# Gate, up and W_down regrouped by every fourth column, and wo's end loaded in quarters, in a decode kernel

## The chip, the cores and the metric

The kernel runs on one core of one Trainium2 chip. The metric is the device time of one execution in microseconds. A comparison runs both kernels in alternation on the same chip. Beside the time, each run gives its span: the time from the first to the last instruction in the records. The profile is of one execution, and its clock starts at the span's start.

## The reference

One decode step of a pre-norm block: two batch elements, one query token each, 32 heads, 8192 cached keys and values for each head, head size 128, then a gated MLP with 512 inputs and 1376 hidden columns. Everything is bf16.

```python
def _A_ref(x, k_cache, v_cache, wq, wo):        # cut: reshapes
    q = (x @ wq).reshape(B, Sq, Hq, Dh)
    scores = jnp.einsum("bhqd,bhkd->bhqk", q, k) * (Dh ** -0.5)
    p = _softmax(scores, axis=-1)
    o = jnp.einsum("bhqk,bhkd->bhqd", p, v)
    return o.reshape(B, Sq, Hq * Dh) @ wo
def _B_ref(x, W_gate, W_up, W_down):
    gate = jnp.einsum("bsd,df->bsf", x, W_gate)
    up = jnp.einsum("bsd,df->bsf", x, W_up)
    h = gate * (gate > 0) * up                  # cut: dtype casts
    return jnp.einsum("bsf,fd->bsd", h, W_down)
h = x + _A_ref(_layernorm(x), k_cache, v_cache, wq, wo)
h2 = h + _B_ref(_layernorm(h), W_gate, W_up, W_down)
```

## The kernel before

The caches are 268 MB (2 x 2 x 32 x 8192 x 128 elements of two bytes), so the kernel is a long stream of loads. A loop of 16 rounds handles four heads a round: VectorE multiplies keys with the query and adds them up, ScalarE takes the exponentials, TensorE applies the values. Behind the last cache load the SyncE queue holds wo, W_gate, W_up and W_down, in the order in which they are needed. The loads of that tail:

```python
for k in range(NGR):                            # wo in two halves of 2 MB
    s.dma("sp", f"dwo{k}", lambda k=k, r0=r0: sync.dma_start(
        out=wo_sb[:, k * JG:(k + 1) * JG, :]..., in_=A_wo[r0:r0 + NS * G * Dh, :]...
# ... gate, up (3 of 4 chunks), up (the last chunk)
for f, r in blocks:                             # W_down: 4, 4 and 2 rows for each of 128 partitions
    s.dma("sp", f"dwd{f}", lambda f=f, r=r: sync.dma_start(
        out=wd_sb[:, f:f + r, :].rearrange("p r n -> p (r n)"),
        in_=B_W_down[f * P:(f + r) * P, :].rearrange("(p r) n -> p (r n)", r=r)), ...
s.dma("sp", "dwdl", lambda: sync.dma_start(out=wd_l, in_=B_W_down[FULL:F, :]), ...)   # last 96 rows
```

Gate and up are matrix products with the two batch elements in the stationary operand, made in three column tiles of 512 columns (the third overlaps the second); then their product is turned into columns and multiplied with W_down:

```python
def mlp_in(g, ps, c0, c1):
    for c in range(c0, c1):
        for j in range(FT):                     # FT = 3
            last = pe.matmul(out=ps[j * Q:(j + 1) * Q, :],
                             lhsT=hd[:, c].rearrange("p a b -> p (a b)"),
                             rhs=wgu[:, g, c, offs[j]:offs[j] + MT], ...)
# ... product, columns_of_act
for f0, r in blocks:
    def fn(f0=f0, r=r):
        for f in range(f0, f0 + r):
            last = y_rows(act_t[:, f, :], wd_sb[:, f, :])     # four matmuls of 128 columns
        return last
    s.op("pe", fn, reads=["act_t", f"wd{f0}"], writes=["y"])
s.op("pe", lambda: y_rows(act_t[0:LASTW, NF, :], wd_l, last=True), ...)
```

The softmax here doesn't subtract the row's maximum and nothing guards it: scores larger than these inputs give would overflow.

## Time and profile before

| what | value |
|---|---|
| time, median of 3 runs | 660.19 us (660.06 to 660.62) |
| span of the profiled run | 658.7 us |
| DMA packets of the load queue, share of 16 engines' span | 98.9% |
| VectorE busy | 618.0 us, 94% |
| one round of the loop, by the value loads' landings | 38.70 us |

The first view is the page of the kernel before: busy time, share of the span and instructions of each engine; the busy tenths of the DMA engines in 40 slices; and the queues that moved data, with packets, megabytes and share.

```profile
PE 115.0 (17%) x1234; PEld 47.3 (7%) x1234; DVE 618.0 (94%) x184; ACT 59.4 (9%) x155; POOL 3.8 (1%) x15
...
DMA  9999999999999999999999999999999999999996
...
q1 hardware_dynamic: 6456, 281.06, 98.9%
q8 instruction: 3, 0.05, 0.0%
q14 instruction: 3, 0.02, 0.0%
```

The DMA row is 9 in every slice but the last. VectorE's 94% looks like a second limit, but it is the lesser one: in the loop it keeps up with the loads, and it waits 4.6 us in all for keys. The two small queues at the bottom fetch instructions.

The second view is the chain of waits of the kernel before, the part at the end: start, duration, what it was.

```profile
621.36 22.94 DMA v<-in_A_wo_dram
...
644.43 1.91 PE mm L596 x13
...
646.36 0.73 DVE osb L611
...
648.55 1.76 PE o L654 x12
...
650.72 1.85 PE mm L654 x12
...
652.66 0.69 DVE qrep L674
...
654.12 1.37 PE y L645 x44
...
655.51 0.29 DVE sc L711
```

Read it as a ladder. The second half of wo lands at 644.29; 16 matmuls finish the attention output, VectorE transposes it, gate, up, their product, and 44 matmuls with W_down follow, and at 655.51 the result is cast for the output. No load but wo is in it: in this kernel the end is bound by its own computing. The last of W_down landed at 654.60, in time for the last of the 44 matmuls.

The third view is the timeline of the kernel before: start, duration, engine, line, operation, tiles, shapes, count; in brackets the idle time before and what ended it.

```profile
644.43 1.87 PE L596 MATMUL mm<-v 128*2 128x512 bf16 x16 [3.05 <-DMA v<-in_A_wo_dram]
...
648.42 1.90 PE L654 MATMUL o<-k,sc 128*32 128x512 bf16 x12
...
650.65 1.89 PE L654 MATMUL mm<-k,sc 128*32 128x512 bf16 x12
...
654.12 1.34 PE L645 MATMUL y<-k,v 128*2 128x128 bf16 x44 [0.28 <-ACT v L696]
```

The last line: all 44 matmuls run in one go and wait for ScalarE, not for a load.

### The profile page before, as it was taken

The page shows a single profiled execution, that of the slowest core. Times are in us where ns is not written, and L with a number is a line of the kernel's source. Part 1 is how long each engine was busy: PE and PEld are TensorE (multiplying, and loading weights), DVE is VectorE, ACT ScalarE, POOL GpSimd, SP SyncE. Part 2 cuts the span into 40 slices and gives each one's busy share as a digit, 9 for nine tenths or more (in the row PEclk, how much of TensorE's full clock was granted, in tenths as well). Part 3 has the DMA queues.
Part 4 walks back from the last instruction along what each step waited for, and adds up shares of the span by engine and source line. Part 5 has one row for each costly group of instructions (what it writes and reads, how often), then busy time and mean ns, then how long its engine had stood idle before and what let it go on. Part 6 is the DMA issues. An engine that isn't in the chain of part 4 may idle for free. (4 is left out here: it accounts for less than half of the span.)

```text
span 658.7 us, 3100 instructions
## 1 busy us (share of the span) xinstructions
PE 115.0 (17%) x1234; PEld 47.3 (7%) x1234; DVE 618.0 (94%) x184; ACT 59.4 (9%) x155; POOL 3.8 (1%) x15
## 2 busy tenths in 40 slices
PE   2200302003030110303011030300203030020365
PEld 1000100001010000101000010100001010010122
DVE  1799999999999999999999999999999999999972
ACT  2301010010101001010100101010010101001100
POOL 2000000000000000000000000000000000000000
PEclk9655655656565575656557565565756556575655
DMA  9999999999999999999999999999999999999996
GB/s 378 447 446 414 418 446 442 446 438 394 446 442 442 442 402 438 442 442 442 410 430 442 442 442 414 426 442 442 442 434 406 446 442 438 438 406 442 418 421 248
DMA packets 6474, 281.13 MB, mean 427 GB/s; under 512 B 738, under 2 KB 836, under 8 KB 1348
## 3 DMA queue, kind: packets, MB, share of 16 engines
q1 hardware_dynamic: 6456, 281.06, 98.9%
q8 instruction: 3, 0.05, 0.0%
q14 instruction: 3, 0.02, 0.0%
q10 hardware_dynamic: 12, 0.00, 0.0%
HBM read 281.05 MB, written 0.00 MB: 427 GB/s over the span
## 5 line engine op out<-in xcount | busy, mean ns | idle before, releaser
L364 DVE TENSOR_TENSOR k<-k,qrep 128x32768 bf16<-128x32768 bf16 (+3 forms) x18 | 275.9, 15327 | 4.6 <-DMA k<-in_A_k_cache_dram 4.6
L370 DVE TENSOR_TENSOR k<-k 128x4096 bf16<-128x4096 bf16 (+6 forms) x72 | 267.4, 3714 | 2.5
L406 PE MATMUL o<-v,pm 128*32 128x512 bf16 x960 | 83.9, 526 | 466.9 <-PEq L434 466.9
L383 ACT ACTIVATE pm<-sc 32x256 bf16<-32x256 f32 (+2 forms) x68 | 48.2, 709 | 562.9 <-DVE sc L227 562.1
L406 PEld LDWEIGHTS o<-v,pm 128*32 128x32 bf16 x960 | 35.2, 127 | 515.3 <-issue 508.4
L227 DVE TENSOR_REDUCE sc<-k 128x256 f32<-128x2048 bf16 (+2 forms) x17 | 36.7, 2160 | 0.8 <-PE o L406 0.3
L453 DVE TENSOR_REDUCE osb<-om 128x128 f32<-128x512 f32 x16 | 16.5, 1029 | 0.6
L383 ACT ACTIVATION_READ_ACCUMULATOR pm<-sc 32x1 f32 x68 | 15.8, 233 | 0.0
L349 DVE CAST qrep<-mm 32x512 bf16<-32x512 f32 x4 | 2.8, 696 | 11.1 <-PE mm L333 11.1
L449 DVE TENSOR_TENSOR om<-o,turn_of 128x512 f32<-128x512 f32 x16 | 10.9, 681 | 1.8 <-PE o L406 1.8
L413 PE MATMUL rep<-osb,spread 128*32 128x128 f32 x40 | 3.9, 420 | 48.4 <-DVE osb L453 45.0
L406 PE MATMUL o<-k,pm 128*32 128x512 bf16 x64 | 7.4, 628 | 7.7 <-ACT pm L383 5.3
L333 PE MATMUL mm<-v,om 128*64 128x512 bf16 x32 | 6.6, 572 | 8.7 <-DMA v<-in_A_wq_dram 8.5
L346 ACT ACTIVATE qrep<-mm 32x512 bf16<-32x512 f32 x12 | 7.0, 587 | 9.1 <-PE mm L333 8.9
L611 DVE STREAM_TRANSPOSE osb<-mm 128x512 f32<-128x512 f32 x1 | 0.7, 717 | 6.7 <-PE mm L596 6.7
L413 PEld LDWEIGHTS rep<-osb,spread 128*32 128x32 f32 x40 | 1.4, 146 | 50.9 <-DVE osb L453 46.6
L596 PE MATMUL mm<-v 128*2 128x512 bf16 x32 | 3.7, 620 | 3.0 <-DMA v<-in_A_wo_dram 3.0
L522 POOL TENSOR_TENSOR zm<-zm,zx 128x1 f32<-128x1 f32 x1 | 0.2, 191 | 627.5 <-ACT pm L383 627.5
L333 PEld LDWEIGHTS mm<-v,om 128*64 128x64 bf16 x32 | 2.5, 152 | 12.4 <-issue 10.3
L406 PEld LDWEIGHTS o<-k,pm 128*32 128x32 bf16 x64 | 2.0, 133 | 12.7 <-ACT pm L383 6.7
L301 DVE COPY xc<-st 128x8 f32<-128x8 f32 x1 | 0.2, 165 | 2.6 <-PE st L296 2.6
L654 PE MATMUL o<-k,sc 128*32 128x512 bf16 x12 | 1.9, 628 | 0.0
(81 smaller groups left out, 33.3 us busy)
## 6 DMA issues: line engine op xcount, KB each, us to landing
k<-in_A_k_cache_dram SPq DMA_DIRECT2D x2, 4096.0 KB, 26.8
v<-in_A_wq_dram SPq DMA_DIRECT2D x1, 4096.0 KB, 12.3
k<-in_A_v_cache_dram SPq DMA_DIRECT2D x1, 4096.0 KB, 31.4
v<-in_A_wo_dram SPq DMA_DIRECT2D x2, 2048.0 KB, 20.4
k<-in_A_v_cache_dram SPq DMA_DIRECT2D x1, 3072.0 KB, 38.3
k<-in_B_W_gate_dram SPq DMA_DIRECT2D x1, 1376.0 KB, 14.9
k<-in_B_W_up_dram SPq DMA_DIRECT2D x1, 1032.0 KB, 17.1
k<-in_A_v_cache_dram SPq DMA_DIRECT2D x1, 1024.0 KB, 40.4
```

Of the source, the lines that this page charges most:

```text
L227: s.op("dve", lambda: dve.tensor_reduce(out=out_, in_=in_, axis=axis, op=ALU.add), reads=reads, writes=writes)
L333: last = pe.matmul(out=ps[h * B * Q:(h + 1) * B * Q], lhsT=xnb[:, c].rearrange("p b q -> p (b q)"), rhs=wq_h[:, c, g:g + QP, h0 + h, :], s ...
L346: s.op("act", lambda src=src, dst=dst: act.activation(out=dst, in_=src, func=ACT.Copy), reads=[f"mm{t}"], writes=[key])
L349: s.op("dve", lambda src=src, dst=dst: dve.tensor_copy(dst, src), reads=[f"mm{t}"], writes=[key])
L364: s.op("dve", lambda: dve.tensor_tensor(out=kp, in0=kp, in1=_view(qrep[:, b, i, :], 0, [[0, hi - lo], [1, Dh]]), op=ALU.mult), reads=keys ...
L370: s.op("dve", lambda half=half, width=width: dve.tensor_tensor(out=kp[:, :, 0:half], in0=kp[:, :, 0:half], in1=kp[:, :, half:width], op=AL ...
L383: last = act.activation(out=p_of[ps, lo // TG:hi // TG, :, h], in_=sc[ps, lo:hi].rearrange("p (g t) -> p g t", t=TG), func=ACT.Exp, accum_ ...
L406: last = pe.matmul(out=o[g:g + W2], lhsT=pm[:, t // TG, :], rhs=vs[:, t:t + TG, :].rearrange("p t d -> p (t d)"), start=(t < P // Q * TG), ...
L413: return pe.matmul(out=rep_ps[u * Q:(u + 1) * Q, :], lhsT=spread.rearrange("k h m -> k (h m)"), rhs=osb[:, u, :], start=True, stop=True, s ...
L449: s.op("dve", lambda: dve.tensor_tensor(out=om.rearrange("p (t d) -> p t d", d=Dh), in0=o.rearrange("p (t d) -> p t d", d=Dh), in1=_view(t ...
L453: fn = lambda: dve.tensor_reduce(out=osb[:, u, :], in_=om.rearrange("p (t d) -> p d t", d=Dh), axis=AXIS.X, op=ALU.add)
L596: last = pe.matmul(out=ar_ps[g:g + B], lhsT=oc[:, k, :], rhs=wo_sb[:, k, :], start=False, stop=(k + P // Q >= NK), skip_group_check=True)
```

## The change

The intent is a shorter computing chain at the end. wo's second half is loaded as a half and two quarters, so that only 4 of its 16 matmuls remain after the last landing. Gate and up are made in four column tiles, tile j holding the columns j, j+4, j+8 and so on: 344 instead of 512 columns for each matmul, with nothing done twice. The hidden columns then stand in fours, so W_down is loaded as rows of four. 344 rows of four are 2 x 128 + 32 + 56; the last 56 (224 rows of W_down) go in eight loads of seven partitions each, so that only seven DMA engines carry them. Masks are built on GpSimd, scores have two buffers, the input x is loaded a second time, from ScalarE's queue, and some waits and some small VectorE operations go.

```diff
+    WO = ((0, 0, JG), (1, 0, JG // 2), (1, JG // 2, JG * 3 // 4), (1, JG * 3 // 4, JG))
+    for k, lo, hi in WO:
# ... the loads of wo and the attention matmuls follow these pieces
-        red(head_blk, ident.rearrange("p (h m) -> p h m", h=G), AXIS.X, i, ["head"])
# ... row_of and eye_of likewise: now copies and memsets on GpSimd; sc has two buffers
-    for f, r in blocks:
-        s.dma("sp", f"dwd{f}", ... 
-    s.dma("sp", "dwdl", lambda: sync.dma_start(out=wd_l, in_=B_W_down[FULL:F, :]),
+    s.op("pool", lambda: pool.memset(wd_sb[0:2 * Q, 2 * FT:], 0.0), writes=["wd2"], extra=x_free)
+    load_down("wd0", 0, slice(0, P), 0)
+    load_down("wd1", P, slice(0, P), FT)
+    load_down("wd2c", 2 * P, slice(2 * Q, 3 * Q), 2 * FT)
+    for h in range(2):
+        for m in range(4):
+            rest.append(f"wd2{h}{m}")
+            load_down(rest[-1], 2 * P + Q + h * 4 * NE + m,
+                      slice(h * Q + m, h * Q + m + 4 * NE - 3, 4), 2 * FT, [cleared])
-    for g in range(B * NGR - 1):
-        normalize(*divmod(g, NGR))
# ... one VectorE operation in place of two normalizations
-                                 rhs=wgu[:, g, c, offs[j]:offs[j] + MT],
+                                 rhs=wgu[:, g, c, j:F:FT],          # FT = 4
# ... the y matmuls of h move behind gate
-    for f0, r in blocks:
-    ...
-    s.op("pe", lambda: y_rows(act_t[0:LASTW, NF, :], wd_l, last=True), ...
+    for u in range(2):
+        s.op("pe", lambda u=u: add_y(u, P), reads=["act_t", f"wd{u}"], writes=["y"])
+    s.op("pe", lambda: add_y(2, 3 * Q), reads=["act_l", "wd2", "wd2c"] + rest, writes=["y"])
```

## The prediction

> **What bounds the kernel now.** The DMA engines. The DMA row of the 40 slices reads 9 everywhere but at the end, the queue's packets fill 98.9% of 16 engines' span, 281 MB pass at 427 GB/s, and from the trace's packets at least 16 are in flight at every moment sampled from 530 to 651 us. VectorE is close behind (618.0 us busy, 94%) and waits 4.6 us in all for keys. So in the loop (38.70 us a round by the value loads' landings) a faster VectorE only waits longer: nothing from the second score buffer, the masks on GpSimd, the dropped waits.
>
> **The end** is two races. The chain of waits follows one: second wo load lands 644.29, 16 matmuls 644.43 to 646.3, transpose 646.36, gate 648.42, up 650.65 to 652.54, product 652.66, columns 653.40, ACT copy 653.87, 44 down matmuls 654.12 to 655.49, cast 655.51, then some 3 us of output. The other is DMA: last increments of gate 647.61, up 650.09 and 650.99, W_down 652.49, 653.79, 654.40, 654.60. Three engines are late (last load: 653.93, 653.99, 654.60 against 652.3 to 653.2).
>
> **What the change does there**
> - wo in quarters: 4 instead of 16 matmuls after the last landing; a round of four takes 0.427 us, so 1.28 us less. But 8 KB and 4 KB packets move at 26.2 and 25.0 bytes/ns against 26.7 for 16 KB (packet medians): about +0.24 us on every later landing.
> - Gate and up: four rounds of 344 instead of 512 columns, 0.287 instead of 0.427 us: 0.56 us less each, if reading every fourth column is free. [...] Product and columns shrink by an estimated 0.4 us.
> - The y matmuls of h move behind gate: 0.43 us of PE, hidden while up is awaited.
> - W_down: 48 instead of 44 matmuls (+0.11 us). After the second block the late engines carry 8 KB instead of 22 KB in small packets, 0.33 instead of 0.95 us. The 224 rows cost seven engines 8 x 0.17 us; [...] The trace names no engines; I assume these seven are early ones.
>
> **Sum.** Compute gets some 2.6 us shorter, but runs into the loads: gate waits for its landing (about 647.85), up for 650.3, and the down matmuls, ready by about 653.0 instead of 654.1, stall for the second W_down block, 653.79 + 0.24 = about 654.03. After it 32 matmuls (0.86 us issue, 0.2 drain): cast at about 655.26 instead of 655.51. Only 0.25 us stays; the rest becomes waiting for DMA.
>
> Predicted: 659.9 us, range 659.0 to 660.8 (8 in 10). Faster by over 2%: 1%; within 2%: 98%; slower: 1%.
>
> **What would show it.** Loop round 38.70 as before; attention matmuls after wo 0.6 instead of 1.9 us; gate starting on a DMA, rounds of 0.29 us; a W_down load as the chain's last DMA; y matmuls split by a wait of some 0.8 us; last landing near 654.2.
>
> **What would make it wrong.** [...] one of the seven engines a late one (+1 us); instruction fetches, which I take to be what makes three engines late (16 KB at 27 and 635 us, 8 KB at 177, 199, 638), falling elsewhere (0.3 to 0.6 us either way).

The sum came to 659.9 us, 660.19 less the 0.25 us by which the cast moves.

## The result, and the profile after

The first comparison gave a median of 661.43 us for the changed kernel (660.86 to 661.63, six runs) against 660.39 us for the kernel before (660.06 to 660.85, six runs). The ratio was 1.0014, with a 95% interval of 1.0001 to 1.0027. A ratio here is the mean time of one kernel's fast runs over that of the other's of the same rounds, so not quite the ratio of the medians. A repetition among the experiments gave 1.0011 (0.9997 to 1.0024). By these ratios the change costs 0.7 to 0.9 us, 0.1% of the time; the second interval just holds 1. It was predicted to gain 0.3.

The page after, the lines that answer to those of before:

```profile
PE 114.0 (17%) x1244; PEld 47.1 (7%) x1244; DVE 617.2 (94%) x180; ACT 59.4 (9%) x155; POOL 7.7 (1%) x29
...
DMA  9999999999999999999999999999999999999996
...
q1 hardware_dynamic: 6648, 281.06, 98.9%
q8 instruction: 3, 0.05, 0.0%
q14 instruction: 2, 0.02, 0.0%
```

The same bytes in more packets, a little less VectorE work, and one instruction fetch fewer inside the span. The loop's round is 38.70 us, as before. The chain of waits after, its end:

```profile
627.13 2.30 DVE k L380
641.94 12.88 DMA k<-in_B_W_down_dram
```

The last link of the chain is now a load of W_down. From the moment of its issue the chain goes back through SyncE, which issues the MLP loads one after another from 632.62 us on, to VectorE's work on the last keys, because the MLP weights may only be written into that buffer when the keys have been read. The issuing is not what holds the end: the last eight loads were issued 0.74 us apart but landed 0.18 us apart. The timeline after:

```profile
644.13 0.60 PE L617 MATMUL mm<-v 128*2 128x512 bf16 x4 [0.66 <-DMA v<-in_A_wo_dram]
...
647.55 1.42 PE L676 MATMUL o<-k,sc 128*32 128x344 bf16 x16 [1.16 <-DMA k<-in_B_W_gate_dram]
...
650.00 1.42 PE L676 MATMUL mm<-k,sc 128*32 128x344 bf16 x16
...
652.84 0.39 PE L667 MATMUL y<-k,v 128*2 128x128 bf16 x16 [0.40 <-DMA k<-in_B_W_down_dram]
...
653.95 0.39 PE L667 MATMUL y<-k,v 128*2 128x128 bf16 x16 [0.72 <-DMA k<-in_B_W_down_dram]
...
654.95 0.39 PE L667 MATMUL y<-k,v 96*2 96x128 bf16 x16 [0.61 <-DMA k<-in_B_W_down_dram]
655.40 0.29 DVE L731 CAST sc<-y 128x128 bf16<-128x128 f32 x1 [2.75 <-PE y L667]
```

Nearly every step is shorter, and nearly every step now has a load in its brackets. Step by step, from the starts in the two timelines and the landing of the last piece of wo in the records (644.29 before, 644.08 after):

| step | before, us | after, us |
|---|---|---|
| last wo landing to transpose | 2.07 | 0.69 |
| transpose to gate | 2.06 | 2.78 |
| gate to up | 2.23 | 2.45 |
| up to product | 2.01 | 1.54 |
| product to first W_down matmul | 1.46 | 1.30 |
| first W_down matmul to cast | 1.39 | 2.56 |
| sum | 11.22 | 11.32 |

Attention saves 1.38 us, and the chain is 1.3 us ahead at the first W_down matmul (652.84 against 654.12, of which 0.2 came from wo). Nearly all of it is lost in the last row, in waits for W_down. From the cast to the end of the span it takes 3.65 us after and 3.23 before. Of that, 0.38 us is one thing: VectorE's last drain instruction began 0.49 us after the semaphore instruction in front of it, where it was 0.11 us before (in these profiles the gap is always one or the other).

Here are the landings of the W_down loads, by the last increment of each load's semaphore:

| load | before | after |
|---|---|---|
| first 128 partitions x 4 rows | 652.49 | 652.70 |
| second 128 x 4 rows | 653.79 | 653.90 |
| before: 128 x 2 rows; after: 32 partitions x 4 rows | 654.40 | 654.34 |
| before: 96 rows; after: the eighth seven-partition load | 654.60 | 654.82 |

### The profile page after: what moved, and what is told of

Same layout as the page of the kernel before. It is cut to its first block, busy times and chain, and to the rows that moved or that the text cites. A ratio compares the mean times of both kernels' runs of the same rounds, so it can differ in the third digit from the quotient of the medians.

```text
span 659.0 us, 3129 instructions
## 1 busy us (share of the span) xinstructions
PE 114.0 (17%) x1244; PEld 47.1 (7%) x1244; DVE 617.2 (94%) x180; ACT 59.4 (9%) x155; POOL 7.7 (1%) x29
## 4 chain that ended last, share of the span: by engine, by line
DVE 74%; DMA 24%; SPq 1%; issue 1%; PE 0%
DVE k L374 34%; DVE k L380 33%; DMA k<-in_A_k_cache_dram 22%; DVE sc L229 5%; DMA k<-in_B_W_down_dram 2%; SPq L549 1%; DVE osb L463 1%; DVE om L459 1%; SPq L540 0%; PE y L667 0%; SPq L283 0%; DVE ou L229 0%; DVE sc L731 0%; DVE rep L475 0%; SPq L770 0%
## 5 line engine op out<-in xcount | busy, mean ns | idle before, releaser
L416 PE MATMUL o<-v,pm 128*32 128x512 bf16 x960 | 85.8, 536 | 465.6 <-PEq L444 465.6
```

The source lines that it names most:

```text
L416: last = pe.matmul(out=o[g:g + W2], lhsT=pm[:, t // TG, :], rhs=vs[:, t:t + TG, :].rearrange("p t d -> p (t d)"), start=(t < P // Q * TG), ...
```

## The experiments

A late engine, here, is a DMA engine that ends its share of every load well after the others: in the kernel before, three engines ended the last load at 653.93, 653.99 and 654.60 us, and the others by 653.18.

Three explanations stood after the first look. Theory W: the W_down part costs the time; its last landing is later than before, because loads into few partitions are slow, or because one of the seven engines is a late one. Rival R: the rest of the change costs it, above all fewer VectorE instructions, which may put an instruction fetch on the last drain (the 0.38 us). And within theory W theory P stood against a rival H. Theory P says that packets are slow when several DMA engines write into few, close partitions; H says that the last rows of W_down are slow to read, wherever they are written.

All edits are against the changed kernel unless it says otherwise. "Before" is always the median or mean of nine runs of the kernel before on the same chip: medians 660.59, 660.59, 660.29 and 660.49 us for the four groups of runs.

### First group: repetition, fourteen engines, the fetch moved back, wo alone

The changed kernel again, no edit.

> The changed kernel unchanged, once more, to learn how its executions spread and to get a second trace. If the two profiled executions (658.7 before, 659.0 after) are typical, the changed kernel is 0.3 us slower, not the 1.0 us that the medians say. If the 1.0 us is real, its usual span is 659.5 to 659.8 and this trace, unlike the first, should show what takes the other 0.5 us, in the last 25 us.

Measured: 661.04 us (660.67 to 661.76), ratio 1.0011 (0.9997 to 1.0024), mean +0.59 us. In its profile the last W_down landing was 655.00, the cast 655.59, and the last drain again began 0.49 us after its release. So the loss repeats, with the sign and about the size of the first comparison.

Fourteen engines for the last 56 rows, two loads of 28 partitions:

```diff
-        for m in range(4):
-            rest.append(f"wd2{h}{m}")
-            load_down(rest[-1], 2 * P + Q + h * 4 * NE + m,
-                      slice(h * Q + m, h * Q + m + 4 * NE - 3, 4), 2 * FT, [cleared])
+        rest.append(f"wd2{h}")
+        load_down(rest[-1], 2 * P + Q + h * 4 * NE, slice(h * Q, h * Q + 4 * NE), 2 * FT, [cleared])
```

> The last 224 rows of W_down in two loads of 28 partitions (14 engines each) instead of eight of 7 partitions. Theory A: the seven engines are a bad choice, because one of them is itself late: its eighth row of 4 KB lands 654.82, 0.48 us after the latest engines had finished (654.34). With 14 engines each has four rows, about 0.74 us. If both latest engines are outside the fourteen, the last landing is near 654.35, the cast starts near 654.95 instead of 655.40, the time falls 0.45 us. If one is inside, the last landing is near 655.05 and the time rises 0.2 us. Rival B (instruction fetch of VectorE at the end): no change from this but what the landing gives.

Measured: 661.63 us, ratio 1.0018 (1.0004 to 1.0032). The last landing was 655.53. All three late engines took part in these loads; the two engines that did not are not late. And the packets became slow: a packet took up to 2.1 times its usual time between 651.25 and 653.25. The 28 partitions of each of these loads lie side by side.

Nineteen small VectorE instructions added at the start, so that VectorE has about as many as in the kernel before and its instruction fetches fall where they fell:

```diff
     build_masks()
+    for _ in range(19):
+        s.op("dve", lambda: dve.tensor_copy(zx, eps_t), reads=["eps"], writes=["zx"])
```

> The changed kernel with 19 tiny VectorE copies in the prologue, where VectorE idles, so that it has as many instructions as before. Theory B: the 8 KB instruction fetch that came at 638.6 us before and at the end after moves back into the run, VectorE's last drain comes 0.11 us after its release as before, not 0.49 us, and the span falls by up to 0.35 us, less what the fetch costs a DMA engine near 640 us (up to 0.3 us). Theory A: no change.

Measured: 661.62 us, ratio 1.0019 (1.0005 to 1.0033). The drain's gap was 0.11 us again, so the stall goes with the number of VectorE instructions. Two 8 KB fetches moved with that number too: they were at 177.2 and 659.4 us in the changed kernel and at 63.5 and 638.2 here, which is how they are taken to be VectorE's. Amid the loads such a fetch took 0.31 to 0.33 us in the traces of the kernel before and of the changed kernel. That a fetch is what holds the drain is not shown: the one at 659.4 us began 0.7 us after the held drain had started (658.72), and after the end of the span (659.05). But the time got worse, not better. In its timeline:

```profile
654.16 0.40 PE L669 MATMUL y<-k,v 128*2 128x128 bf16 x16 [0.76 <-DMA k<-in_B_W_down_dram]
656.04 0.39 PE L669 MATMUL y<-k,v 96*2 96x128 bf16 x16 [1.49 <-DMA k<-in_B_W_down_dram]
```

One engine delivered its eight rows of the seven-partition loads at 654.62, 654.81 and so on to 655.91, a row every 0.18 us; the other six were done by 654.19. With the fetch back at 638 us, one of the seven engines is the latest of all. Without it, in the changed kernel, the same loads end at 654.82.

The quarters of wo alone, in the kernel before:

```diff
-    for k in range(NGR):
+    WO = ((0, 0, JG), (1, 0, JG // 2), (1, JG // 2, JG * 3 // 4), (1, JG * 3 // 4, JG))
+    for k, lo, hi in WO:
...
-    attention_rows(NK - JG, NK, False)
+    for k, lo, hi in WO[1:]:
+        attention_rows(k * JG + lo, k * JG + hi, False)
```

> The kernel before with the second wo load in three pieces (8, 4 and 4 columns of rows) and nothing else. As I costed it: transpose 1.3 us earlier, gate then waits for its own landing, the down matmuls for W_down, so the cast comes 0.2 to 0.4 us earlier. If small packets cost what I said, every later landing is 0.24 us later and nothing or little is gained; the changed kernel's trace already says that they do not (last wo landing 644.08, not 644.53).

Measured: 660.32 us, ratio 0.9998 (0.9985 to 1.0012). The transpose started at 644.92 instead of 646.36, but the last W_down landing was 654.58, as before, and the cast came at 655.03, so about 0.5 us was left in this profile and 0.2 us in the mean of the times. The kernel before had that much room and no more before it would meet its last load.

### Second group: which engine, and two repairs

The 56 rows in loads of 7, 6, 5, 4, 3, 3 and 7, 6, 5, 4, 2, 2, 2 partitions, one row for each engine, to see which engine is the late one:

```diff
-    for h in range(2):
-        for m in range(4):
+    for h, counts in ((0, (7, 6, 5, 4, 3, 3)), (1, (7, 6, 5, 4, 2, 2, 2))):
+        at_row = 0
+        for m, k in enumerate(counts):
```

> A measurement, not a version: the 56 partition rows of the last 224 rows in loads of 7, 6, 5, 4, 3, 3 and 7, 6, 5, 4, 2, 2, 2 partitions[...]. Theory A says that one of the [...] engines is late by 0.7 us or more [...]. A load that includes it has one increment that stands apart from the others by that much; the first k whose load has no such increment names the engine. If no load shows one, the lateness belongs to the partitions or the row stride and not to an engine.

Measured: 661.93 us, one run, state unknown; an engine that takes part in all thirteen loads carries thirteen rows here, so the time itself says nothing. How many engines carry a load is read from its semaphore: in the trace of the changed kernel that of the first seven-partition load has one record at 637.82 us, long before its data moves, and then the seven increments from 652.43 to 653.52 us, as data lands. In the nested kernel the increments agree with the counts of partitions; loads over eight and sixteen partitions are counted alike below, one engine to a partition. The loads of the first half show how a late engine is found, last increments in us:

```
load over 7 partitions: 653.81      over 4: 654.39
load over 6 partitions: 653.99      over 3: 654.05
load over 5 partitions: 654.19      over 3: 654.22
```

The latest increment climbs by about 0.2 us a load down to four partitions, and then falls back: the late engine is in the load of four and not in the loads of three. It is called engine 3 from here on: counted from 0, the one that the load over four adds to those over three. The number is a name only: no trace says which of the chip's engines it is.

Four VectorE copies of the queries given to ScalarE, and the last normalizations to GpSimd, so that VectorE's fetch does not fall on the end at all (the page counts five VectorE instructions fewer, 175 against 180):

```diff
-                if h == 0 or b == 0:
+                if True:                          # copy on ScalarE
...
-        normalize(B - 1, k)
+        s.op("pool", lambda k=k, g=g: pool.tensor_scalar_mul(...
```

> The changed kernel with 5 fewer VectorE instructions (the four query copies that it shares with ScalarE in the prologue go to ScalarE, one normalization to GpSimd). Theory B: [...] no 8 KB fetch comes at the end and the last drain follows its release by 0.11 us instead of 0.49: the span falls by 0.38 us. In the earlier padded run the fetch came back at 638 us [...]: cast 656.49. Here neither: cast 655.4 to 655.6, span near 658.7 to 658.9. If the drain stays at 0.49 us, the stall is not the fetch.

Measured: 661.18 us, ratio 1.0012 (0.9998 to 1.0026). The drain's gap was 0.11 us and there was no fetch at 638 us, as meant; the last one was recorded at 660.6 us, 1.6 us after the span. Counting those of its sequencer, VectorE has 193 instructions in every trace with the stall, and 189 or 212 in every trace without. The mean span was 0.30 us shorter than the first group's repetition (659.06 against 659.36), but the mean time was not (661.24 against 661.17). The stall is real in the span and does not explain the time.

The last 88 rows of four spread evenly: 80 over sixteen engines and 8 over eight, no memset.

```diff
-    load_down("wd2c", 2 * P, slice(2 * Q, 3 * Q), 2 * FT)
-    for h in range(2): ...
+    load_down("wd2c", 2 * P, slice(0, 80), 2 * FT)
+    load_down("wd2", 2 * P + 80, slice(80, 88), 2 * FT)
```

> The changed kernel with the last 88 rows of four of W_down in one load of 80 partitions (16 engines, 5 rows each) and one of 8 partitions (8 engines), no seven-engine loads, no clearing. Theory A: the last landing no longer depends on which engine is in the seven, but the latest engines carry 5 rows of 4 KB instead of 2, 0.55 us more: last landing near 654.8, cast near 655.4, like the fastest run of the changed kernel and 0.2 to 0.6 us better than its usual runs. VectorE's end stall stays, 0.38 us. So 660.6 to 661.0 us.

Measured: 661.11 us, ratio 1.0010 (0.9996 to 1.0023), last landing 655.30. Packets took 1.6 to 2.3 times as long between 651.75 and 653.25. Sparing no engine is no worse than the change's choice, and no better. This run also says what the slow packets cost: after the second block each engine carries 20 or 24 KB, about the 22 KB of the kernel before, and the first up load landed at about the same time (650.16 against 650.09), yet in these two profiles the second block landed 0.82 us later (654.61 against 653.79) and the last load 0.70 us later.

### Third group: the same rows into other partitions

Three kernels load the same last 88 rows of four, into the same 88 partitions, and differ in which partitions one load writes. In the first, six loads of (up to) 16 neighbouring partitions; in the second, five loads of every fifth partition of 80 and one of the last 8; in the third, eleven loads of eight partitions, four apart (the last three loads three apart):

```diff
+    # packed
+    load_down(rest[-1], 2 * P + 16 * m, slice(16 * m, min(16 * m + 16, 88)), 2 * FT)
+    # spread
+    load_down(rest[-1], 2 * P + (m if m < 5 else 80), slice(m, 80, 5) if m < 5 else slice(80, 88), 2 * FT)
+    # eight engines
+    for lo, hi, step in ((0, 32, 4), (32, 64, 4), (64, 88, 3)):
+        for m in range(step):
+            load_down(rest[-1], 2 * P + lo + m, slice(lo + m, hi, step), 2 * FT)
```

> The last 88 rows of four of W_down in five loads of 16 partitions that lie side by side (0-15, 16-31, ...) and one of 8; every engine carries one row of 4 KB per load. Theory P [...]: in the changed kernel every packet between 651.3 and 652.4 us took up to twice its usual 0.164 us [...]. [...] the last landing is 655.5 or later. Rival H: the last rows of W_down, or small loads, are slow to read whatever they are written to: then this run and the spread one have the same packet times.

> The same rows, bytes, loads and engines as the packed run, but each load writes every fifth partition (0, 5, ... 75)[...]. Theory P: packets at 1.3 to 2 times 0.164 us, last landing at least 1 us earlier than packed (near 654.8 to 655.2). Rival H: no difference from packed.

> The same 88 rows in eleven loads of 8 partitions, every fourth partition for the first 64 rows [...] (every third partition for the last 24). Theory P: the slow stretch at 651.3 to 652.4 us is gone (packets within 1.1 of usual until the last three loads), the latest engines finish the second block near 653.3 instead of 653.9, and the last landing is [...] near 654.3: cast near 654.8, span near 658.5 with VectorE's end stall still in it. Rival H: slow stretch stays, landing near 655.

The reason for these three: if close partitions are what makes packets slow, loads over the same partitions should be slowest side by side, faster five apart, and undisturbed four apart with eight engines. Measured, as the mean packet time over the usual time of a packet of its size (0.164 us for 4 KB), in quarter-microseconds:

| kernel | partitions of one load | worst ratio | when slow, us | last landing, us | median, us | ratio of times (95%) |
|---|---|---|---|---|---|---|
| packed | side by side | 2.65 | 651.25 to 653.5 | 655.76 | 661.94 | 1.0023 (1.0008 to 1.0039) |
| spread | every fifth, last load side by side | 2.04 | 651.25 to 653.5 | 655.44 | 661.37 | 1.0013 (0.9998 to 1.0029) |
| eight engines | every fourth, last three loads every third | 1.35 | 652.5 to 653.25 | 654.75 | 661.27 | 1.0015 (1.0001 to 1.0028) |

In the third kernel the ratio was 0.97 to 1.0 until 652.5, while its first eight loads were moving, and rose only with the loads three apart. H is refuted for the first 64 of the 88 rows: the same rows from the same addresses moved at full speed in the third kernel and at half speed or less in the other two. Theory P fits, but it is not isolated. In all three kernels row number i goes to partition number i, so which rows are read together changes along with which partitions are written together, and the third has eight engines in these loads where the others have sixteen. And one trace does not fit the simple form: in the nested kernel every packet was at its usual time from 653.0 us on (ratio 0.97 to 0.99), while loads over seven to three neighbouring partitions were still landing. Here is what the slow packets do to the W_down matmuls, first in the packed kernel, then in the eight-engine kernel:

```profile
653.77 0.40 PE L661 MATMUL y<-k,v 128*2 128x128 bf16 x16 [1.17 <-DMA k<-in_B_W_down_dram]
654.99 0.59 PE L661 MATMUL y<-k,v 128*2 128x128 bf16 x16 [0.83 <-DMA k<-in_B_W_down_dram]
656.00 0.60 PE L661 MATMUL y<-k,v 88*2 88x128 bf16 x16 [0.41 <-DMA k<-in_B_W_down_dram]
```

```profile
652.48 0.39 PE L662 MATMUL y<-k,v 128*2 128x128 bf16 x16 [0.23 <-ACT v L710]
653.77 0.40 PE L662 MATMUL y<-k,v 128*2 128x128 bf16 x16 [0.89 <-DMA k<-in_B_W_down_dram]
654.89 0.39 PE L662 MATMUL y<-k,v 88*2 88x128 bf16 x16 [0.73 <-DMA k<-in_B_W_down_dram]
```

In the packed kernel even the first block is late, 653.77 against 652.48, although that block is the same load in both: the late engines were still moving it when the early engines' last loads made every packet slow. So the early engines' last loads are paid for by the late engines' earlier ones.

The changed kernel itself has this too. Its packets took 1.64 to 2.04 times as long between 651.5 and 652.25, and in the kernel before never more than 1.27 times. By elimination it is probably the load into 32 neighbouring partitions that does it, for the seven-partition loads, into partitions four apart, land at full pace, 0.18 us a row, with a ratio of 0.97 to 1.03 from 652.5.

The eight-engine kernel with the edit of fewer VectorE instructions:

```diff
# the eight-engine kernel, and:
-                if h == 0 or b == 0:
+                if True:                          # copy on ScalarE
-        normalize(B - 1, k)
+        s.op("pool", lambda k=k, g=g: pool.tensor_scalar_mul(...
```

> The eight-engine version with 5 fewer VectorE instructions as well: both causes taken away. Span 0.38 us less than the eight-engine version, near 658.1, against 658.5 of before; time 660.2 to 660.5, so the change would at last be worth 0.2 us or so over before.

Measured: 661.14 us, ratio 1.0013 (1.0000 to 1.0027), last landing 654.85, no stall at the drain. Against the eight-engine kernel the mean span is 0.44 us shorter (659.00 against 659.44) and the mean time is the same (661.16 against 661.20). The crowding was not all gone: with the last three loads, three partitions apart, packets took up to 2.05 times as long from 652.5 to 653.25, where the trace of the eight-engine kernel had 1.35. So taking away the stall and most of the crowding does not bring the time back: here eight engines carry eleven rows each, 11 x 0.164 = 1.8 us. That the late engine 3 is one of them is not shown.

### Fourth group: the two halves of the change, each alone

The whole change without its MLP part (constants, W_down loads and MLP code of before), and the kernel before with only that part of the change:

```diff
# rest only, against the changed kernel (cut; the lines of the columns and of the y matmuls follow)
-    load_down("wd0", 0, slice(0, P), 0)           # and the other W_down loads and the memset
+    for f, r in blocks:
+        s.dma("sp", f"dwd{f}", ...
-                                 rhs=wgu[:, g, c, j:F:FT],
+                                 rhs=wgu[:, g, c, offs[j]:offs[j] + MT],
# MLP only, against the kernel before: the same lines the other way round
```

> The changed kernel with gate, up and W_down of the kernel before (three tiles of 512, loads into 128 and 96 partitions): all the rest of the change. Theory W (the W_down loads cost what is left): span 658.3 as with wo alone, plus 0.38 of VectorE's end stall, so 658.6 to 658.8, and no stretch of slow packets. Rival R (the rest of the change costs it): 659.1 or more.

> The kernel before with gate and up in four tiles and the new W_down loads, nothing else. Theory W: slow packets near 651.3 to 652.4, the fetch at 638 us makes engine 3 of the seven late as in the padded run, last landing 655.5 to 656, span 659.6 to 660.0 without an end stall. Rival R: no slower than before, 658.1 to 658.5.

Measured: the rest alone 660.40 us, ratio 0.9998 (0.9985 to 1.0012), with a mean of 660.46 against 660.46 of the kernel before: 0.00 us. The MLP part alone 661.66 us, ratio 1.0017 (1.0004 to 1.0031), mean +1.11 us, and +1.10 us in the mean span. The interval of the rest alone is wide, 0.9 us either way, but the runs of the two halves do not overlap: 660.01 to 660.77 us and 661.30 to 661.78. The rest alone has the stall at the drain (gap 0.49 us) and no cost that shows; the MLP part alone has no stall (0.11 us) and costs more than the whole change. W holds and R falls. Gate and up in four tiles were not run apart from the new W_down loads, since the loads follow from the order of the columns; that it is the loads is read from the waits. The timeline of the MLP part alone:

```profile
644.17 1.88 PE L602 MATMUL mm<-v 128*2 128x512 bf16 x16 [2.76 <-DMA v<-in_A_wo_dram]
...
648.16 1.42 PE L660 MATMUL o<-k,sc 128*32 128x344 bf16 x16 [0.45 <-DVE sc L637]
...
653.65 0.39 PE L651 MATMUL y<-k,v 128*2 128x128 bf16 x16 [0.21 <-DMA k<-in_B_W_down_dram]
655.53 0.39 PE L651 MATMUL y<-k,v 96*2 96x128 bf16 x16 [1.49 <-DMA k<-in_B_W_down_dram]
```

It stands ready at 654.1 after the second block and then waits 1.49 us for the seven-partition loads. In them six engines end by 653.93, and the seventh delivers rows from 654.09 to 655.39, 0.19 us apart. In the kernel before, an engine has eight packets of 2 KB and six of 1 KB left after the second block, 22 KB in all; here one of the seven has two of 4 KB and then eight of 4 KB, 40 KB.

That the MLP part alone costs more than the whole change also has its place: the whole change has fewer VectorE instructions, so the 8 KB fetch at 638 us (0.325 us) is gone, and the seven's late engine is less late: in the changed kernel two engines outside the seven end the second block after it (653.83 and 653.90 us, when all of the seven had landed their first row by 653.52). Giving the fetch back, in the first group, gave the loss back too: mean span +1.41 us over before, against +0.85 us for the change beside it.

The quarters of wo once more, and the rest of the change with the edit of fewer VectorE instructions, so with neither the stall nor the fetch at 638 us:

```diff
 # rest only, and:
-                if h == 0 or b == 0:
+                if True:                          # copy on ScalarE
...
-        normalize(B - 1, k)
+        s.op("pool", lambda k=k, g=g: pool.tensor_scalar_mul(...
```

> The kernel before with the second wo load in three pieces, a second time: span 658.34 the first time against 658.51 of before. If the gain is real the two together show 0.2 us, otherwise not.

> r12 with VectorE's instructions reduced as in r6, so that no fetch comes at 638 us [...]: span 0.38 us below r12, near 658.2; and [...] perhaps 0.1 us below that one.

Measured: wo's quarters 660.33 us, ratio 0.9999 (0.9985 to 1.0013), mean -0.06 us where it was -0.20 in the first group; a gain by them alone is not settled. The rest with fewer VectorE instructions 660.19 us (659.91 to 660.60), ratio 0.9995 (0.9982 to 1.0009), mean span 657.88 against 658.44 us. Its timeline at the end:

```profile
653.08 0.90 PE L663 MATMUL y<-k,v 128*2 128x128 bf16 x32 [0.28 <-ACT v L714]
654.19 0.55 PE L663 MATMUL y<-k,v 128*2 128x128 bf16 x12 [0.22 <-DMA k<-in_B_W_down_dram]
654.79 0.29 DVE L729 CAST sc<-y 128x128 bf16<-128x128 f32 x1 [1.80 <-PE y L663]
```

This is the best version that came out: wo in quarters, the lighter VectorE program and W_down as before. It is some 0.9 to 1.2 us faster than the changed kernel (mean -0.27 us against the kernel before of the same chip, where the changed kernel had +0.59 and +0.94) and 0.3 us by the medians faster than the kernel before. The interval for that last comparison holds 1, so a gain over the kernel before is not settled by the times; by the span it is 0.56 us. It too now ends on W_down's last landing, 654.33, so computing saved before that would only become waiting.

## Why the prediction was wrong

It said 659.9 us with a range to 660.8. The two medians of the changed kernel were 661.43 and 661.04. Point by point:

- "The DMA engines" bound the kernel, and the loop stays at 38.70 us: right. The lighter VectorE program, the second score buffer and the masks on GpSimd moved nothing in the loop; everything but the MLP part together changed the mean time by 0.00 us.
- Reading every fourth column is free: nearly right. The column tiles of a round run side by side: in the kernel before, a round of three matmuls of 512 columns (gate) started every 0.42 us, and a round of four (wo) every 0.41. In the changed kernel a round of four matmuls of 344 columns started every 0.30 us, and 0.42 x 344 / 512 = 0.28. So no more than 0.02 us a round was lost, where twice the time would have been 0.56.
- Computing gets some 2.6 us shorter: right. From the table and the timelines it is 1.38 us in attention, 0.48 and 0.47 us in gate and up, and about 0.4 us from the product to the columns (1.46 us before, 1.06 in the MLP part alone, where no load is waited for there). It became waiting, as said: gate, up and all three parts of the W_down matmuls now wait for loads.
- Smaller wo packets cost 0.24 us on every later landing: not seen. The last piece of wo landed at 644.08 instead of 644.29 us, but in that kernel the fetch at 638 us was gone as well. In the kernel with wo's quarters alone, which kept the fetch, it landed at 644.23 us. Over all traces with the quarters it was between 643.87 and 644.52.
- **The step that failed is W_down.** The prediction put it as "After the second block the late engines carry 8 KB instead of 22 KB in small packets, 0.33 instead of 0.95 us. The 224 rows cost seven engines 8 x 0.17 us", and "I assume these seven are early ones". From it came a last stop at the second block, about 654.03, and a cast at 655.26. The second block did land at 653.90. But the last landing was 654.82 and 655.00 in the two profiles and the cast 655.40 and 655.59. One of the seven engines is a late one: the nested loads show it, in the load over four partitions (last increment 654.39) and not in those over three (654.05). For it, the 8 x 0.17 us (measured 8 x 0.18 to 0.19) come after its own late second block and its two rows of the third, and not beside them. In the kernels with the fetch at 638 us it ends at 655.39 (MLP part alone) or 655.91 us (fetch given back). The prediction named this as the thing that could make it wrong, with "+1 us"; the MLP part alone cost 1.11 us. That the two agree so well is partly luck, for the next point is in the 1.11 us too.
- A second part of the same term was not thought of: while loads into few, close partitions are in flight, the packets of all engines take up to twice as long (2.04 in the changed kernel); that the closeness of the partitions is the reason is argued, not isolated, and how it would act is not shown. The late engines' third load, priced at 0.33 us, ended 0.44 us after the second block.
- "Instruction fetches ... falling elsewhere (0.3 to 0.6 us either way)": right that it happened. The fetch at 638 us (638.57 in the kernel before) went, one was recorded after the end of the span instead (659.43), and the last drain was held for 0.38 us; that the one causes the other is not shown.

Why an engine is late is only partly shown. That the fetch at 638 us makes engine 3 later is inferred from three kernels in which the fetch and that engine's landings moved together (655.91 and 655.39 us with it, 654.82 without); no trace names the engine that carries a fetch. Which two engines are the other late ones is open. The loads over fourteen engines hold them, and the loads over eight do not (in the eight-engine kernel two engines ended the second block at 653.70 and 653.72, when the eight engines of those loads had all delivered their first row of them by 652.71). Open too is why the stall at the drain shows in the span and not in the measured time: the time less the span was 2.0 to 2.1 us for the kernel before, 1.76 to 1.86 us for kernels with the changed MLP part and the stall, but also 1.81 us for the one with nineteen instructions more and no stall, 1.98 us for the rest alone, 2.03 us for the MLP part alone, and 2.16 to 2.31 us for those with fewer VectorE instructions. The mean spans differ from the profiled ones by up to 0.5 us either way (659.5 against 659.05 for the changed kernel), and what no profile shows was not traced further.

## What to carry to other kernels

When computing at the end is shortened until it waits for a load, the next microsecond belongs to the latest DMA engine (here 655.39 us, when six others were done by 653.93), so find out which engines are late before giving a few of them extra rows; loads nested by partition count, each with its own semaphore, show it in one run. Lay the last loads out as the kernel's full loads are, or try partitions four apart (packets at 0.97 to 1.0 times the usual in the eight-engine kernel's first eight loads), and look at the time of single packets, not only at landings: here the packed loads delayed the loads queued before them (the first block's matmuls started at 653.77 instead of 652.48 us). And split a change into its parts before tuning it: here one half cost 1.1 us and the other nothing, and four repairs of the costly half each brought nothing back.
